# Weights on ScalarE's queue, zero products from the start, and new instruction sequences, in a gated linear attention with a maxout FFN behind it

## Chip, cores and metric

The kernel runs on one core of one Trainium2 chip. The metric is device time in microseconds; the median of three runs of the kernel before is 151.06 us (150.87 to 151.34). Engines are named as in the profile: PE (TensorE, matrix products), PEld (its weight loads), DVE (VectorE), ACT (ScalarE), POOL (GpSimd) and SP (SyncE, which here only requests transfers). Transfers can be requested from SP and from ACT; SPq and ACTq are the rows of these requests.

## What is computed

For each of 4 batches and 8 heads a 48 × 48 state is decayed row by row and gets an outer product added at each of 768 steps; its product with q is the attention's output. The outputs of all heads side by side (3072 tokens of 384) go through a maxout of three matrices and a last matrix.

```python
B, H, S, D = (4, 8, 768, 48)
for t in range(S):
    state = alpha[:, :, t, :, None] * state + einsum('bhd,bhe->bhde', k[:, :, t], v[:, :, t])
    y[:, :, t] = einsum('bhd,bhde->bhe', q[:, :, t], state)
x = y.transpose(0, 2, 1, 3).reshape(B * S, H * D)          # 3072 x 384
h = maximum(maximum(x @ w1, x @ w2), x @ w3)               # 3072 x 768
out = h @ w_out                                            # 3072 x 384
```

Inputs and output are float32. alpha lies between 0.8 and 1.0.

## The kernel before

The work is cut into 24 *units*: 128 time steps of one batch, all 8 heads. Unit u is time block u // 4 of batch u % 4, and two units make a load group n (`load`, line 301): alpha, q, k and v of both, in one transfer each, or one per unit for the first four groups. In the names of the steps, "load a 0 8" is alpha of unit 1, "load a 1 0" that of unit 2.

For each unit the attention is done in chunk form: logarithm of alpha on ACT (`decay`, L402); running sums of it along time by a product with a triangular matrix on PE ("cums", L442); two exponentials of these on ACT (ep and en, L447 and L450); q and k scaled by them on POOL or DVE (L454); v scaled on ACT or POOL (L461, L464); both turned on PE ("turn", L483) and copied to SBUF (L490); "scores" on PE (L499), masked on DVE ("LA", L504); outputs from scores, v and the carried state Z on PE ("outs", L542 and L545), scaled to 16 bits (xb, L556 and L558), turned ("x turn", L572) and copied (xT, L577). `state` carries Z on.

The FFN uses that max(a, b, c) = a + max(0, b − a, c − a). So the kernel casts w1 and w_out to 16 bits on ACT (L333), makes wd = w2 − w1 and w3 − w1 on DVE or POOL (`subs`, L341), and folds w1·w_out into one 384 × 384 matrix: w1 is turned on PE ("w1 turn", L366), copied by ACT (w1T, L372), multiplied with w_out on PE ("fold", L383), and copied by ACT (w1o, L390). Then `ffn` needs two expansions ("grow", L642) per token instead of three, a relu on ACT (L653), a max on DVE (L658), and one contraction ("shrink", L678) over the 384 x's and the 768 h's together. Single units are taken for the first four and last two, pairs else.

Each weight matrix comes in two pieces, columns 0 to 255 and 256 to 767 (rows for w_out): 384 KB and 768 KB (`weights`, L327). All four matrices are requested by SP. "weights g p" is piece p of matrix g in the order w1, w2, w3, w_out.

The program is recorded as *steps*, each with the engines that may do it, and then issued in the order of a written table `ORDER`; `PICK` says where a step takes its second engine, and `BANKS` which of 8 PSUM banks each intermediate gets. So every engine does its work in exactly the order of that table, and waits for data where it must. The tables were the result of a planner that is no part of the kernel.

"zeros" are products of a state tile that holds zeros, written to a PSUM bank that nothing reads (`warm`, L586). There are 27, the first of which waits for k of unit 1 (`reads` of `("qk", hq[u], w)`); they keep TensorE busy where it has nothing else.

Of the kernel before, what the change touches and what calls it, by code (L numbers as in the profile page):

```python
# [17 lines left out]
SIG = 128.0  # L18

# [4 lines left out]
WARM = (1, 1, 27)  # L24
# [55 lines left out]
)  # L80
BANKS = (
# [9 lines left out]
)  # L91
PICK = {
# [8 lines left out]
}  # L101


TRANSFERS = ("load", "weights", "cross", "store")
BEHIND = mybir.DependencyInfo(mybir.DependencyClass.NoSync, mybir.DependencyReason.DATA)
HARD, HARD_LOAD, HARD_LATE, LATE_FROM = 0.5, 1.8, 1.5, 3

# [662 lines left out]
```

## Time and profile before

| | before |
|---|---|
| median of 3 runs | 151.06 us (150.87 to 151.34) |
| the profiled execution | 150.59 us |
| its span, first to last instruction | 148.8 us |
| busy: PE / DVE / ACT / POOL | 133.9 / 106.9 / 90.5 / 52.5 us |
| read from HBM / written | 23.69 / 4.72 MB |

Line numbers in the profile are those of the listing above. "out<-in" names the tiles an instruction writes and reads. The busy time of PE counts pipelined products up to a modelled end; the columns of a stretch are its length, each engine's busy time with the count of its instructions, the granted clock of TensorE (1.00 is full), the busy share of the 16 DMA engines, and GB/s. The share can pass 1, since packets overlap.

### The profile page before, as it was taken

The numbers are of one execution on the slowest core, as the hardware profiler recorded it, in microseconds if no ns is written. First come the engines' busy times: TensorE is split into PE (matmuls) and PEld (weight loads), VectorE is DVE, ScalarE is ACT, GpSimd is POOL, SyncE is SP. The second block draws the span as 40 slices with busy tenths as digits, with TensorE's granted clock in tenths as the row PEclk, the third lists the DMA queues.
The fourth block names the chain that finished last, engine by engine and source line by source line (L and its number), as shares of the span: only waits on it lengthen the run. The fifth ranks groups of instructions, "written<-read, shape, count | busy, mean of one in ns | idle before, by whom it ended". The sixth has DMA issues, their size and how long they took to land.

```text
span 148.8 us, 4162 instructions
## 1 busy us (share of the span) xinstructions
PE 133.9 (90%) x1683; PEld 104.6 (70%) x1683; DVE 106.9 (72%) x186; ACT 90.5 (61%) x184; POOL 52.5 (35%) x75
## 2 busy tenths in 40 slices
PE   0575297999999999999999999999999999999991
PEld 0233266968787886888787797787878877689781
DVE  7239318487998898979697779998578878584140
ACT  3531976948667587797746686745475844554331
POOL 0050041202523414840597709448029290170000
PEclk9999659999999999999999999999999999999999
DMA  5999999999999999999999999899998999704322
GB/s 115 205 225 322 202 341 269 283 267 173 223 208 219 237 220 210 248 184 250 266 266 263 185 197 250 163 215 269 177 232 160 243 325 189 147 4 131 109 82 79
DMA packets 116131, 31.07 MB, mean 209 GB/s; under 512 B 109712, under 2 KB 114960, under 8 KB 116112
## 3 DMA queue, kind: packets, MB, share of 16 engines
q1 hardware_dynamic: 83888, 21.17, 69.7%
q10 hardware_dynamic: 32224, 9.64, 28.7%
q8 instruction: 13, 0.21, 0.6%
q14 instruction: 6, 0.05, 0.1%
HBM read 23.69 MB, written 4.72 MB: 191 GB/s over the span
## 4 chain that ended last, share of the span: by engine, by line
PE 85%; SPq 5%; DMA 4%; ACT 2%; DVE 2%; issue 0%; ACTq 0%
PE psum L642 33%; PE psum L678 24%; PE psum L499 5%; PE psum L483 4%; SPq L308 4%; DMA vn<-in_v_dram 4%; PE psum L545 3%; PE psum L572 3%; PE psum L442 3%; PE psum L542 2%; PE psum L604 2%; PE psum L383 2%; PE psum L586 2%; PE psum L412 1%; DVE wd L341 1%; ACT w1h L333 1%
## 5 line engine op out<-in xcount | busy, mean ns | idle before, releaser
L642 PE MATMUL psum<-xT,wd 128*128 128x256 f16 (+1 forms) x540 | 54.4, 251 | 0.9 <-DVE wd L341 0.9
L642 PEld LDWEIGHTS <-wd 128*128 128x128 f16 x540 | 42.9, 98 | 6.9 <-DVE wd L341 1.7
L658 DVE TENSOR_TENSOR hT<-psum,hT 128x512 f16<-128x512 f32 (+1 forms) x39 | 24.3, 644 | 10.3 <-PE psum L642 4.7
L504 DVE TENSOR_TENSOR LA<-psum,c 128x1024 f16<-128x1024 f32 x24 | 28.6, 1219 | 3.1 <-PE psum L499 2.5
L653 ACT ACTIVATE hT<-psum 128x512 f16<-128x512 f32 (+1 forms) x39 | 21.5, 570 | 14.6 <-PE psum L642 13.6
L678 PE MATMUL psum<-wo,hT 128*128 128x384 f16 (+1 forms) x150 | 27.7, 320 | 0.0
L617 POOL TENSOR_TENSOR Z<-U,G 48x192 f16<-48x192 f32 x29 | 16.4, 572 | 12.5 <-DVE U L611 11.4
L678 PEld LDWEIGHTS <-hT 128*128 128x128 f16 x150 | 14.5, 98 | 8.9
L454 POOL TENSOR_TENSOR qk<-qn,ep 128x384 f16<-128x384 f32 x11 | 10.9, 998 | 15.1 <-ACT ep L447 13.3
L678 PE MATMUL psum<-w1o,xT 128*128 128x384 f16 (+1 forms) x75 | 15.8, 319 | 0.0
L450 ACT ACTIVATE en<-psum 128x384 f32<-128x384 f32 x24 | 11.9, 495 | 4.3 <-PE psum L442 3.8
L402 ACT ACTIVATE la<-an 128x384 f16<-128x384 f32 (+1 forms) x16 | 10.8, 689 | 5.7 <-DMA an<-in_alpha_dram 5.7
L454 POOL TENSOR_TENSOR qk<-kn,en 128x384 f16<-128x384 f32 x8 | 8.3, 1042 | 16.6 <-ACT en L450 12.7
L556 ACT ACTIVATE xb<-psum,c 128x384 f16<-128x384 f32 x16 | 9.1, 582 | 8.0 <-PE psum L545 5.8
L447 ACT ACTIVATE ep<-psum 128x384 f32<-128x384 f32 x24 | 11.7, 496 | 2.6 <-DVE qk L454 0.9
L693 ACT COPY ob<-psum 128x384 f32<-128x384 f32 (+1 forms) x18 | 8.3, 468 | 7.8 <-PE psum L678 5.1
L442 PE MATMUL psum<-la,c 128*128 128x384 f16 x24 | 7.8, 347 | 5.6 <-ACT la L402 5.5
L461 ACT ACTIVATE v<-vn,c 128x384 f16<-128x384 f32 x14 | 8.3, 614 | 6.2 <-DMA vn<-in_v_dram 6.2
L545 PE MATMUL psum<-v,LA 128*128 128x48 f16 x192 | 11.1, 186 | 0.0
L611 DVE TENSOR_TENSOR U<-psum,Z 128x384 f32<-128x384 f32 x16 | 8.5, 551 | 3.1 <-PE psum L604 2.5
L545 PEld LDWEIGHTS <-LA 128*128 128x128 f16 x192 | 9.8, 98 | 0.6 <-issue 0.2
L464 POOL TENSOR_SCALAR v<-vn,c 128x384 f16<-128x384 f32 x10 | 6.3, 635 | 9.4 <-DMA vn<-in_v_dram 9.0
(61 smaller groups left out, 189.6 us busy)
## 6 DMA issues: line engine op xcount, KB each, us to landing
out_dram<-ob ACTq DMA_DIRECT2D x20, 192.0 KB, 3.3
an<-in_alpha_dram SPq DMA_DIRECT2D x7, 384.0 KB, 6.6
ws<-in_moe_w_dram SPq DMA_DIRECT2D x3, 768.0 KB, 6.1
kn<-in_k_dram SPq DMA_DIRECT2D x5, 384.0 KB, 6.5
vn<-in_v_dram ACTq DMA_DIRECT2D x5, 384.0 KB, 6.6
an<-in_alpha_dram SPq DMA_DIRECT2D x8, 192.0 KB, 4.0
kn<-in_k_dram SPq DMA_DIRECT2D x8, 192.0 KB, 4.4
qn<-in_q_dram ACTq DMA_DIRECT2D x4, 384.0 KB, 5.3
```

What stands on the lines that cost most here:

```text
L402: lambda e, lo=lo * H, hi=hi * H: nc.scalar.activation(out=la[:, lo:hi, :D], in_=an[:, lo:hi, :], func=AFT.Ln, scale=1.0 / CDEC),
L442: nc.tensor.matmul(live[Lk], tri, la[:, hs, :D], start=True, stop=True)
L447: lambda e: nc.scalar.activation(out=ep, in_=live[Lk], func=AFT.Exp),
L450: lambda e: nc.scalar.activation(out=en, in_=live[Lk], func=AFT.Exp, scale=-1.0),
L454: lambda e, w=w, x=x, d=d: engines[e].tensor_mul(qk[:, w, :, :D], ld[x][n % LOADED][:, hs], d),
L504: lambda e: nc.vector.tensor_mul(LA.rearrange("p a b t -> p (a b) t"), live[Ak].rearrange("p a (b t) -> p (a b) t", t=P), maskA.unsqueeze( ...
L545: nc.tensor.matmul(yp[:, 2 * j + p, :], LA[:, p, j, :], v16[:, 2 * j + p, :], start=(cb == 0), stop=True, skip_group_check=True)
L617: lambda e, rows=rows, cols=cols: engines[e].tensor_mul(Zn[rows, :, cols], (Us[u % 3] if cb else live[pk])[rows, :, cols], G[rows, i * NP: ...
L642: nc.tensor.matmul(live[gk][:, jj, :], wd[:, kt, g, j * P:(j + 1) * P], xT[:, kt, :], start=(kt == 0), stop=(kt == NFT - 1))
L653: lambda e, h=h, gk=gk: nc.scalar.activation(out=h, in_=live[gk], func=AFT.Relu),
L658: lambda e, h=h, gk=gk: nc.vector.tensor_max(h, live[gk], h),
L678: nc.tensor.matmul(live[ok][:, cols], a[:, i * P:(i + 1) * P], w[:, cols], start=(kt == 0), stop=(kt == nk - 1))
```

## The change

Five edits, made together.

- `weight_options` gets ACT as second engine, and `PICK` takes it for all eight weight pieces. They are requested in the order w1 large, w_out small, w1 small, w_out large, w2 large, w2 small, w3 large, w3 small, between ACT's own instructions.
- The loads on SP start with q of unit 0, alpha of units 0, 1 and 2, k of 0, alpha of 3; all of units 0 and 1 comes before the rest of units 2 and 3. Units 2 and 3 (third and fourth) are worked on after the first eight expansions, and the three fold steps stand ahead of the first expansion.
- `warm` is called before unit 0's outputs, makes 44 zero products instead of 27, and the first depends on nothing but its zeros.
- The tile of zeros is the first that DVE clears, ahead of the other tiles.
- `ORDER`, `BANKS` and `PICK` are replaced as wholes. POOL does 81 steps of the table instead of 71, DVE 159 instead of 166.

The diff without the tables:

```diff
-WARM = (1, 1, 27)
+WARM = 44
...
 def weight_options(share, cast):
     if cast:
         return [("POOL", 0.6 + 0.4 * share, 0, 3.7 * share, 0.2)]
-    return [("SP", HARD, 0, 3.25 * share + 0.1, 0.6)]
+    return [("SP", HARD, 0, 3.25 * share + 0.1, 0.6), ("ACT", 0.45, 0, 3.25 * share)]
...
     hq, ht = rotate(QKS, MORE[0]), rotate(QKTS, MORE[1])
+    nc.vector.memset(Zs[1][0], 0.0)
     for t in las:
         nc.vector.memset(t[:, :, D:], 0.0)
     for t in qks[:QKS]:
         nc.vector.memset(t[:, :, :, D:], 0.0)
-    for zz in Zs:
-        for t in zz:
-            nc.vector.memset(t, 0.0)
+    for t in Zs[0] + Zs[1][1:]:
+        nc.vector.memset(t, 0.0)
...
-    def warm(u, w, count):
+    def warm(count):
...
             plan.step(f"zeros {i}", [("PE", 0.163)], 90.0, zeros,
                       banks=[("wm", 0)] if i == 0 else [],
-                      reads=([("qk", hq[u], w)] if u >= 0 else []) if i == 0 else [("wm", 0)],
+                      reads=[("wm", 0)] if i else [],
                       writes=[("wm", 0)] if i in (0, count - 1) else [])
...
-            if u == WARM[0]:
-                warm(*WARM)
+            if u == 0:
+                warm(WARM)
```

Of the tables, the first line of `ORDER`, by numbers of steps:

```diff
-    4, 8, 9, 5, 6, 0, 10, 12, 34, 7, 32, 1, 11, 2, 123, 65, 127, 82, 84, 128, 129, 83, 64, 131,
+    2, 0, 4, 8, 1, 12, 78, 34, 65, 64, 140, 40, 32, 113, 85, 94, 86, 87, 126, 66, 116, 68, 105,
```

What stands on ScalarE before, around the two casts of w1 (w1h) on whose end TensorE's turns of w1 wait; ws0 is w1, v1 and v2 are scaled v, ep and en exponentials, xb the attention's output in 16 bits:

```order
L402 ACTIVATE la0_82<-an0_66 128x8x48
L461 ACTIVATE v1_101<-vn0_78,c32_62 128x384
L402 ACTIVATE la1_83<-an1_67 128x8x48
L450 ACTIVATE en0_88<-psum_177 128x384
L447 ACTIVATE ep0_85<-psum_177 128x384
L333 CAST w1h_148<-ws0_150 128x3x512
L461 ACTIVATE v2_102<-vn1_79,c32_62 128x384
L333 CAST w1h_148<-ws0_150 128x3x256
L447 ACTIVATE ep0_85<-psum_177 128x384
L490 COPY qkT0_107<-psum_177 128x1024
L556 ACTIVATE xb1_116<-psum_177,c32_62 128x384
L372 COPY w1T_149<-psum_177 128x768
```

What stands there now (ws1 to ws3 are w2, w3 and w_out; lines are two higher in the new kernel):

```order
L335 CAST w1h_148<-ws0_150 128x3x512
L329 DMA ws3_153<-in_moe_w_out_dram 128x4x384
L329 DMA ws1_151<-in_moe_w2_dram 128x3x512
L335 CAST w1h_148<-ws0_150 128x3x256
L420 ACTIVATE e0_141<-psum_177,c32_62 128x16
L449 ACTIVATE ep2_87<-psum_177 128x384
L329 DMA ws1_151<-in_moe_w2_dram 128x3x256
L374 COPY w1T_149<-psum_177 128x768
L329 DMA ws2_152<-in_moe_w3_dram 128x3x512
L335 CAST wo16_155<-ws3_153 128x768
L329 DMA ws2_152<-in_moe_w3_dram 128x3x256
L374 COPY w1T_149<-psum_177 128x768
```

Five requests of weights came in between, both scalings of v and the copy of a turned unit went to other engines, and the small cast of w_out (wo16) moved up from behind the first relus.

What stands on VectorE before, from the last masking ahead of the first subtraction (wd) to the last; ws1 and ws2 are w2 and w3:

```order
L504 TENSOR_TENSOR LA0_112<-psum_177,c16_61 128x1024
L577 COPY xT0_120<-psum_177 128x3x128
L341 TENSOR_TENSOR wd_154<-ws1_151,w1h_148 128x3x512
L577 COPY xT0_120<-psum_177 128x3x128
L454 TENSOR_TENSOR qk3_94<-qn1_71,ep0_85 128x8x48
L490 COPY qkT3_110<-psum_177 128x1024
L504 TENSOR_TENSOR LA0_112<-psum_177,c16_61 128x1024
L341 TENSOR_TENSOR wd_154<-ws2_152,w1h_148 128x3x512
L341 TENSOR_TENSOR wd_154<-ws2_152,w1h_148 128x3x256
```

What stands there now:

```order
L506 TENSOR_TENSOR LA0_112<-psum_177,c16_61 128x1024
L506 TENSOR_TENSOR LA1_113<-psum_177,c16_61 128x1024
L343 TENSOR_TENSOR wd_154<-ws1_151,w1h_148 128x3x512
L579 COPY xT0_120<-psum_177 128x3x128 x2
L343 TENSOR_TENSOR wd_154<-ws2_152,w1h_148 128x3x512
L343 TENSOR_TENSOR wd_154<-ws2_152,w1h_148 128x3x256
```

The subtraction from w2 stands ahead of both x's, and nothing of the fourth unit is left between the subtractions: its product with q went to GpSimd, its copy and its masking went behind the first four maxima.

More of the change, by code (lines that the diff above doesn't have):

```diff
@@ L18 @@
 SIG = 128.0
+TRANSFERS = ("load", "weights", "cross", "store")
+BEHIND = mybir.DependencyInfo(mybir.DependencyClass.NoSync, mybir.DependencyReason.DATA)
 NBANKS = 8
@@ L35 @@
 ORDER = (
[44 rows of a table removed]
[44 rows of a table added]
 )
 BANKS = (
[9 rows of a table removed]
[9 rows of a table added]
 )
 PICK = {
[8 rows of a table removed]
-}
-TRANSFERS = ("load", "weights", "cross", "store")
-BEHIND = mybir.DependencyInfo(mybir.DependencyClass.NoSync, mybir.DependencyReason.DATA)
[10 rows of a table added]
+}
 HARD, HARD_LOAD, HARD_LATE, LATE_FROM = 0.5, 1.8, 1.5, 3
```

120 rows, old and new, of tables (BANKS, ORDER, PICK) are left out of this document.

## Prediction

> **What bounds the kernel now.** I read the page first, then stretches of the span, then the chain that ended last. The page:
>
> ```profile
> span 148.8 us, 4162 instructions
> PE 133.9 (90%) x1683; PEld 104.6 (70%) x1683; DVE 106.9 (72%) x186; ACT 90.5 (61%) x184; POOL 52.5 (35%) x75
> PE 85%; SPq 5%; DMA 4%; ACT 2%; DVE 2%; issue 0%; ACTq 0%
> ```
>
> TensorE is busy for 90% of the span and holds 85% of the last chain; no other engine comes near. Where are the missing 10%? The stretches, with TensorE's busy time, its granted clock and the DMA share:
>
> ```profile
> core 0: us, PE busy (x), PEclk, DMA share, GB/s
> 0.00:5.50 5.50, 0.00 (x0) 1.00 0.73 143
> 5.50:9.40 3.90, 3.78 (x12) 1.00 1.10 217
> 9.40:13.50 4.10, 3.00 (x38) 1.00 1.02 290
> 13.50:17.70 4.20, 0.00 (x0) 0.79 1.03 216
> 17.70:22.10 4.40, 4.39 (x44) 0.50 1.02 328
> 22.10:25.70 3.60, 2.71 (x42) 0.91 1.15 288
> 25.70:33.80 8.10, 8.07 (x104) 1.00 0.99 266
> 33.80:145.80 112.00, 111.95 (x1449) 1.00 1.01 200
> ```
>
> From 25.7 to 145.8 TensorE idles for 0.08 us in all. So the time is decided by how much of its work is left at 25.7, and everything before is a front in which TensorE is empty, or busy with zero products, or at clock 0.50, while the DMA share is 1.0 and more from 5.5 on. The chain through this front:
>
> ```profile
> 8.65 5.77 DMA vn<-in_v_dram
> ...
> 14.51 0.61 ACT v L461
> ...
> 16.29 1.37 ACT w1h L333
> ...
> 17.71 0.82 PE psum L366 x6
> ...
> 23.97 1.68 DVE wd L341
> ...
> 25.69 1.18 PE psum L642 x18
> ...
> 27.03 0.17 PE psum L572 x3
> ...
> 28.91 0.16 PE psum L586
> 29.07 0.45 PE psum L483 x8
> ...
> 30.34 0.36 PE psum L499 x8
> 30.70 3.03 PE psum L383 x18
> ...
> 35.60 0.20 PE psum L545 x8
> ```
>
> A load of v, queued on SP with a weight piece, lets ScalarE go on at 14.51; it casts w1, TensorE turns it (L366), VectorE subtracts w1 from w2 (L341), and at 25.69 the first expansion (L642) starts. The lower rows give the price of each TensorE step at full clock; the product w1·w_out (L383) costs 3.03 and comes after five expansions now.
>
> **The change, part by part.** *What TensorE has done when its expansions start.* Up to its first expansion the new order holds the three products of L383 (3.03) more than the old, and the third unit's turn 0.45, scores 0.36, outputs 0.20 and x turn 0.17 less: 3.03 − 1.18 = 1.85 us ahead. Behind that point stand five zero products instead of four: 0.16 back. All else after it is the same work in another order. So the new kernel ends where the old one does if its first expansion starts at 25.69 + 1.85 − 0.16 = 27.4, provided TensorE stays full afterwards; each microsecond earlier is a microsecond gained. The term to find is that start.
>
> *The transfers.* Rates while loads alone, then a weight piece alone, are moved, and two waits on loads:
>
> ```profile
> 6.00:9.00 3.00, 1.00 1.08 211
> 10.50:11.90 1.40, 1.00 0.99 369
> ```
>
> ```profile
> 4.96 0.94 ACT L402 ACTIVATE la<-an 128x384 f16<-128x384 f32 x2 [2.05 <-DMA an<-in_alpha_dram]
> ...
> 8.79 0.52 ACT L402 ACTIVATE la<-an 128x384 f16<-128x384 f32 x1 [0.69 <-DMA an<-in_alpha_dram]
> ```
>
> A load of one unit is 196.6 KB, at 211 GB/s 0.93 us; a weight piece of 786 KB takes 2.13 at 369, the smaller of 393 KB 1.07. The second load is awaited at 4.96 and the sixth at 8.79: the n-th lands at 3.1 + 0.93 n. (By this the ninth load behind a large piece lands at 13.6; the row has 14.51, so the fit may be 0.9 early.) The DMA engines are full either way, so putting the weights on a second queue makes no bytes faster; it changes who goes first. How two queues share is not seen with weights in this trace. Bounds: the weights wait for all loads in flight, or they push ahead of all loads. I take turns, one transfer each, and both ends move the start below by about a microsecond. The first large piece of w1 goes ahead of the fourth load, so a of the third unit lands at 3.1 + 4 × 0.93 + 2.13 = 9.0, and of the fourth unit (sixth load) at 10.8. ScalarE requests w_out's small and w1's small piece behind the logarithm of 9.0: the latter lands after eight loads at 3.1 + 7.4 + 2.13 + 2 × 1.07 = 14.8. In the same way w_out's large piece lands at 17.9, w2's large piece at 20.9, its small one at 22.9, w3's at 26.0 and 28.0.
>
> *ScalarE's row of work.* Its prices:
>
> ```profile
> 6.46 0.49 ACT L450 ACTIVATE en<-psum 128x384 f32<-128x384 f32 x1 [0.57 <-PE psum L442]
> ...
> 16.18 1.47 ACT L333 CAST w1h<-ws 128x1536 f16<-128x1536 f32 x1
> ...
> 18.06 0.83 ACT L333 CAST w1h<-ws 128x768 f16<-128x768 f32 x1
> ...
> 21.44 0.80 ACT L372 COPY w1T<-psum 128x768 f16<-128x768 f16 x1
> ...
> 25.20 0.30 ACT L418 ACTIVATE e<-psum,c 128x16 f32<-128x16 f32 x1
> ...
> 26.79 1.46 ACT L333 CAST wo<-ws 128x1536 f16<-128x1536 f32 x1
> ...
> 29.43 0.86 ACT L333 CAST wo<-ws 128x768 f16<-128x768 f32 x1
> ```
>
> Logarithm at 9.0 (half of 0.94), 0.57 for the cumulative product, five exponentials at 0.49 and one logarithm: the large cast of w1 runs from about 12.9 to 14.4. The small cast waits for 14.8. From there: 0.83, e 0.30, an exponential 0.49, w1T 0.80, cast 0.86, w1T 0.80, exponential 0.49, w1T 0.80, cast 1.46, together 6.8: at 21.6 w_out stands in 16 bits and L383 can start. TensorE then has 3.03 + two x turns 0.34 + outputs 0.20 + four zero products 0.64 = 4.2 before its first expansion: 25.8. The subtraction from w2 (1.68 from 20.9) is long done, so the cover that hides it is the product of L383. The third matrix is not covered so well: 26.0 + 1.68, and about half of that for the small piece after 28.0, ends at 28.9, while four expansions at 0.5 (1.18 for two and a bit of overlap) reach 27.8 and two more 28.8: 0.15 lost.
>
> *Requests on ScalarE.* How long a request holds its issuer:
>
> ```profile
> 10.77 2.87 SPq L308 DMA_DIRECT2D vn<-in_v_dram  x1
> ...
> 16.63 0.49 SPq L308 DMA_DIRECT2D vn<-in_v_dram  x1
> ```
>
> ```profile
> 58.65 0.40 ACTq L308 DMA_DIRECT2D kn<-in_k_dram  x1
> ```
>
> On ScalarE 0.40, beside the instruction started just before it (a cast, an exponential, a copy), so seven of the eight requests cost nothing. The last, w3's small piece, is made with four others of its queue still on their way, as SP's was at 10.77, and behind it wait the copies of w1T, the cast of w_out and all that follows. Bounds 0 and 2.4 (2.87 − 0.49); nearer the lower end, since the first of the four lands at 17.9, just when the request is due: 0.4. SP is rid of eight requests, worth nothing while the DMA engines are full.
>
> *Zero products from the first microsecond.* Six run at once, then TensorE waits for the first logarithm; the rest fill gaps. At half clock:
>
> ```profile
> 6.22 3.06 PE L586 MATMUL psum<-Z 128*128 128x384 f16 x9
> ```
>
> About 0.32 each instead of 0.16. Between the large cast of w1 and L383 stand 19 of them with three turns of w1 (half of 0.82 each at full clock), two unit turns, two scores and one output: 19 × 0.16 + 3 × 0.41 + 2 × 0.45 + 2 × 0.36 + 0.20 = 6.1 us at full clock, from 14.4 to 20.5, which ScalarE's work to 21.6 hides. If the clock stays halved until 20, 5.6 us do only 2.8 of it, and L383 starts at 20 + 3.3 = 23.3, 1.7 late. Bounds 0 and 1.7; I take 0.35, nearer the lower end: the trace shows full clock after 3.9 us without a pause (5.5 to 9.4), but also 0.50 after 4.2 idle us and through the 4.4 busy us from 17.7.
>
> Sum: 25.8 + 0.15 + 0.4 + 0.35 = 26.7 against 27.4, a gain of 0.7 us: span 148.1. The profiled execution took 150.59 for its span of 148.8 and the median of the runs is 151.06, so 149.9 for a like execution and 150.4 for a median.
>
> **The rivals.** *Clock (slower).* The six early zero products last 6 × 0.32 = 1.9 us, then comes a pause of some 3 (the logarithm needs the third load, after 5.9); from 9 to 13 TensorE is busy in pieces, and idle again for over a microsecond until the cast at 14.4 is through. If full clock needs 3.4 to 3.9 unbroken microseconds, it comes only near 20, L383 starts 1.7 us late as above, and the first expansion moves to 26.7 − 0.35 + 1.7 = 28.05, 0.65 behind 27.4: 151.7. [...] For the rival: the pauses; against: from 14.4 on TensorE has no pause left. It decides if the clock is still 0.5 at 19.
>
> *Late third and fourth unit (slower).* With the weights in turn, the fourth unit's q is the fifteenth load: 3.1 + 15 × 0.93 + 12.8 for all weights = 29.9, and its v, the twentieth, lands at 34.5. Now it is earlier:
>
> ```profile
> 27.83 0.97 DVE L454 TENSOR_TENSOR qk<-qn,ep 128x384 f16<-128x384 f32 x1 [0.17 <-DMA qn<-in_q_dram]
> ```
>
> GpSimd makes both products of this unit now, after one another and before v of the third. TensorE's own work reaches the fourth turn at about 34.5 and its outputs at 38, so I expect this to pass by 1 to 2 us; if loads are served behind weights, or the fit is 0.9 early as above, each later unit's turn waits 0.5 to 1, and the loads of the sixth unit, asked by ScalarE between its own work, repeat it. Price 1 to 3 us off the gain: 151.4 to 153.4.
>
> *More gain.* No clock trouble, no held request, weights ahead: first expansion at 25 to 25.8, a gain of 1.6 to 2.4, 148.7 to 149.5.
>
> **How the numbers follow.** What a measurement can tell from no change is 0.3%, 0.45 us: faster is below 150.6, slower above 151.5. The forecast has 0.45 (149.5 to 151.2: two thirds faster, the rest same and a little), more gain 0.12, the clock 0.16, late units 0.27. Faster: 0.33 + 0.12 + 0.02 = 0.47. Same: 0.12 + 0.03 = 0.15. Slower: 0.13 + 0.25 = 0.38. The range reaches from the middle of "more gain", 148.8, to the end of the late units, 153.4. Both signs are likely; the forecast's own range is 149.5 to 151.2.
>
> **What would show it.** In the new trace, whose lines are two higher: L385 before the first L644, starting near 22, and the first L644 between 25.8 and 27.4; casts of w1 from 12.9 and of w_out ending near 21.6; no idle microsecond of TensorE after that. The clock rival is right if PEclk is 0.5 until about 20 and the zero products last 0.32 there; the late units, if TensorE waits behind GpSimd's products (L456) or v (L466) between 30 and 60. A held request shows as an ACTq row of L329 over 1 us. If TensorE is full from 26 on and the time is still not shorter, my count of the work ahead is wrong.

## The result, and the profile after

The changed kernel is slower: 154.8 us median (154.29 to 156.48) against 151.2 (150.87 to 151.34), ratio 1.029, 95% interval 1.023 to 1.035. On a second chip it took 154.9 against 152.1, ratio 1.020 (1.015 to 1.026). The ratios here and below leave out executions more than 1.5% above the fastest of their kernel, four of the six in e1. The profiled execution took 154.41, its span is 3.8 us longer than before. The page of the changed kernel, its first lines and the chain by engine:

```profile
span 152.6 us, 4192 instructions
PE 138.7 (91%) x1700; PEld 106.5 (70%) x1700; DVE 104.9 (69%) x179; ACT 88.8 (58%) x181; POOL 63.2 (41%) x85
PE 73%; DVE 10%; DMA 8%; ACT 3%; issue 2%; SPq 1%; POOL 0%; ACTq 0%; DVEq 0%; POOLq 0%
```

TensorE was on the last chain for 85% of it and is now for 73%; VectorE came from 2 to 10. The share of busy time, 91%, hides this, since the zero products count as busy. The front in the chain that ended last (start, duration):

```profile
12.90 1.37 ACT w1h L335
...
21.29 1.23 DVE LA L506
...
23.27 0.97 PE psum L385 x6
...
27.69 4.05 DVE wd L343 x2
```

The large cast of w1 runs from 12.9, as reckoned. But the product w1·w_out (L385) starts behind VectorE's masked copy LA of unit 1, at 23.1 and not near 22, and the first expansion at 27.22. Behind it the chain goes at once to VectorE, to the subtraction of the third matrix. The stretches from there on, TensorE alone:

```profile
core 0: us, PE busy (x), PEclk, DMA share, GB/s
27.20:36.00 8.80, 7.59 (x105) 1.00 1.01 200
36.00:45.00 9.00, 8.11 (x139) 1.00 1.19 222
45.00:60.00 15.00, 14.67 (x212) 1.00 1.18 216
60.00:80.00 20.00, 19.24 (x253) 1.00 1.10 203
80.00:149.00 69.00, 68.68 (x857) 1.00 0.90 179
```

The differences add to 3.5 us of idle time, where the old kernel had 0.08 from its first expansion on. What ended it (us in total, times, longest), from 27.3 to 149:

```profile
PE psum L644 <- DVE wd L343: 1.2, 2, 0.7
PE psum L574 <- DVE xb L560: 0.8, 1, 0.8
PE psum L501 <- DVE qkT L492: 0.6, 1, 0.6
PE psum L547 <- POOL v L466: 0.3, 1, 0.3
PE psum L485 <- DVE Z L619: 0.3, 1, 0.3
PE psum L544 <- DVE Z L619: 0.2, 1, 0.2
```

In the old kernel the same view has no row at all from 26.5 to 145.8. To weigh kernels against each other I also use a count of my own, called the excess: for each step of TensorE the time from its start to the start of the next, less what the quickest steps of its kind take, summed from the first expansion to the last step. It is 3.2 us before and 7.2 after; 1.5 of it stands at the third matrix, 1.2 at the zeros tile (42.8 and 43.7), 0.5 at v of unit 4 (49.0), 0.9 at unit 8's output (69.6). It is larger than the idle times of the list, as it also has pauses too short for the list and what slower steps lose. With that the loss closes: start 27.22 − 25.69 = +1.53, useful work left −1.95, one zero product more +0.17, excess +4.06, together 3.81.

Three of these places in the rows. VectorE's subtraction of the third matrix (start, duration, count at the end), in the changed kernel:

```profile
27.60 4.12 DVE L343 TENSOR_TENSOR wd<-ws,w1h 128x1536 f16<-128x1536 f32 x2
```

GpSimd at the same time, in the same timeline:

```profile
27.43 1.00 POOL L456 TENSOR_TENSOR qk<-qn,ep 128x384 f16<-128x384 f32 x1 [1.19 <-DMA qn<-in_q_dram]
28.39 2.52 POOL L456 TENSOR_TENSOR qk<-kn,en 128x384 f16<-128x384 f32 x1
30.87 1.72 POOL L456 TENSOR_TENSOR qk<-qn,ep 128x384 f16<-128x384 f32 x1
```

And the subtraction in the kernel before:

```profile
31.95 2.62 DVE L341 TENSOR_TENSOR wd<-ws,w1h 128x1536 f16<-128x1536 f32 x2
```

The two subtractions take 4.12 beside GpSimd's products and took 2.62 before; the products take 2.52 and 1.72 instead of 1.00. The zeros tile and v of unit 4, in TensorE's timeline of the changed kernel:

```profile
42.60 0.33 PE L588 MATMUL psum<-Z 128*128 128x384 f16 x1
...
43.74 0.61 PE L485 MATMUL psum<-c,qk 128*128 128x128 f16 x8 [0.31 <-DVE Z L619]
44.93 0.40 PE L501 MATMUL psum<-qkT 48*128 48x128 f16 x8 [0.58 <-DVE qkT L492]
...
49.56 0.21 PE L547 MATMUL psum<-v,LA 128*128 128x48 f16 x2 [0.33 <-POOL v L466]
```

The zero product at 42.60 reads the tile that the state Z of unit 0 is to overwrite. So VectorE's Z waits for it, as VectorE's timeline shows:

```profile
42.97 0.72 DVE L619 TENSOR_TENSOR Z<-psum,G 48x192 f16<-48x192 f32 x2 [1.21 <-PE psum L588]
```

Behind Z in VectorE's row stands the copy qkT for which TensorE waits.

### The profile page after: what moved, and what is told of

Same layout as the page of the kernel before. It is cut to its first block, busy times and chain, and to the rows that moved or that the text cites. A ratio compares the mean times of both kernels' runs of the same rounds, so it can differ in the third digit from the quotient of the medians.

```text
span 152.6 us, 4192 instructions
## 1 busy us (share of the span) xinstructions
PE 138.7 (91%) x1700; PEld 106.5 (70%) x1700; DVE 104.9 (69%) x179; ACT 88.8 (58%) x181; POOL 63.2 (41%) x85
## 3 DMA queue, kind: packets, MB, share of 16 engines
HBM read 23.69 MB, written 4.72 MB: 186 GB/s over the span
## 4 chain that ended last, share of the span: by engine, by line
PE 73%; DVE 10%; DMA 8%; ACT 3%; issue 2%; SPq 1%; POOL 0%; ACTq 0%; DVEq 0%; POOLq 0%
PE psum L644 24%; PE psum L680 21%; PE psum L485 5%; DMA an<-in_alpha_dram 4%; DMA kn<-in_k_dram 4%; PE psum L501 4%; PE psum L547 3%; DVE LA L506 3%; PE psum L588 3%; DVE wd L343 3%; PE psum L574 2%; PE psum L444 2%; PE psum L544 2%; PE psum L606 2%; PE psum L385 2%
## 5 line engine op out<-in xcount | busy, mean ns | idle before, releaser
L644 PE MATMUL psum<-xT,wd 128*128 128x256 f16 (+1 forms) x540 | 53.1, 251 | 1.4 <-DVE wd L343 1.2
L644 PEld LDWEIGHTS <-wd 128*128 128x128 f16 x540 | 42.8, 98 | 6.5 <-DVE wd L343 1.5
L660 DVE TENSOR_TENSOR hT<-psum,hT 128x512 f16<-128x512 f32 (+1 forms) x39 | 24.4, 644 | 7.1 <-PE psum L644 4.9
L466 POOL TENSOR_SCALAR v<-vn,c 128x384 f16<-128x384 f32 x16 | 9.9, 622 | 35.7 <-DMA vn<-in_v_dram 29.3
L619 POOL TENSOR_TENSOR Z<-U,G 48x192 f16<-48x192 f32 x23 | 12.0, 527 | 13.9 <-DVE U L613 11.7
L456 POOL TENSOR_TENSOR qk<-qn,ep 128x384 f16<-128x384 f32 x12 | 12.7, 1059 | 10.6 <-ACT ep L449 6.0
L456 POOL TENSOR_TENSOR qk<-kn,en 128x384 f16<-128x384 f32 x14 | 15.5, 1113 | 1.0 <-ACT en L452 0.9
L588 PE MATMUL psum<-Z 128*128 128x384 f16 x44 | 13.5, 422 | 1.1 <-DVE Z L279 1.1
L558 ACT ACTIVATE xb<-psum,c 128x384 f16<-128x384 f32 x14 | 8.2, 583 | 6.4 <-PE psum L547 5.9
L579 ACT COPY xT<-psum 128x384 f16<-128x384 f16 x16 | 7.4, 480 | 7.4 <-PE psum L574 7.4
```

Source lines behind the costliest of these rows:

```text
L456: lambda e, w=w, x=x, d=d: engines[e].tensor_mul(qk[:, w, :, :D], ld[x][n % LOADED][:, hs], d),
L588: nc.tensor.matmul(live["wm"], zero[:, :P], zero, start=True, stop=True)
L619: lambda e, rows=rows, cols=cols: engines[e].tensor_mul(Zn[rows, :, cols], (Us[u % 3] if cb else live[pk])[rows, :, cols], G[rows, i * NP: ...
L644: nc.tensor.matmul(live[gk][:, jj, :], wd[:, kt, g, j * P:(j + 1) * P], xT[:, kt, :], start=(kt == 0), stop=(kt == NFT - 1))
L660: lambda e, h=h, gk=gk: nc.vector.tensor_max(h, live[gk], h),
```

## The experiments

Four theories were open. The order: the loss lies in the places just named, where the new sequences put a step too late or two engines against each other. The queue: weights on ScalarE's queue push the loads back. The clock: TensorE's clock comes up late. And the zero products cost or bring something by themselves. All edits are to the changed kernel unless said otherwise; a number in `ORDER` is a step, and `PICK` sends a step to its second engine.

**e1_no_late_zeros.** The five zero products behind the first expansion.

```diff
-plan.step(f"zeros {i}", [("PE", 0.163)], 90.0, zeros,
+plan.step(f"zeros {i}", [("PE", 0.163)], 90.0, zeros if i not in (10, 34, 22, 42, 43) else lambda e: None,
```

> The changed kernel without the five zero products that stand behind the first expansion (they change no output). Theory, the new sequences lose the time in places that can be named, and these products are one: they take 5 x 0.16 = 0.8 us of a full TensorE, and the last two read the zeros tile that Z 0 0 on VectorE is to overwrite, which the trace shows as waits of 0.48 and 0.75 us at 42.8 and 43.7: the run ends 1.2 to 2.0 us earlier, near 153. Rival, the weights on ScalarE's queue push the loads back and TensorE waits for data whatever the products do: no more than 0.3 us earlier. Rival, the products keep the clock up: without them the clock falls after 27 and the run is longer.

Ratio 1.010 (0.997 to 1.023), times from 151.7 to 156.1. The profiled execution is one of the longer ones, and shows why they spread. TensorE's timeline from 24 to 30:

```profile
26.44 0.41 PE L547 MATMUL psum<-v,LA 128*128 128x48 f16 x8 [2.75 <-POOL v L466]
...
29.84 1.36 PE L644 MATMUL psum<-xT,wd 128*128 128x128 f16 x20
```

Its stretches there (length, busy and instructions, granted clock, DMA share, GB/s):

```profile
24.00:26.00 2.00, 0.00 (x0) 1.00 1.13 262
26.00:28.00 2.00, 1.56 (x13) 0.65 0.59 119
28.00:30.00 2.00, 2.00 (x11) 0.50 1.02 203
```

TensorE was early, waited 2.75 us for v of unit 0, and then had half its clock for 3.4 us (26.6 to 30.0). Behind the first expansion the waits of 0.48 and 0.75 at the zeros tile are gone: VectorE's Z, at 43.29, has no idle time before it, and the rows of 0.6 for qkT and 0.3 for Z are missing from TensorE's list. So this part of the theory holds by the trace; the time alone doesn't settle it.

**e2_sub_early.** VectorE's larger third-matrix subtraction (47) ahead of the transposed copy of unit 0 (125).

```diff
-309, 305, 125, 10, 9, 16, 13, 14, 11, 18, 20, 17, 15, 21, 47, 46, 298,
+309, 305, 47, 125, 10, 9, 16, 13, 14, 11, 18, 20, 17, 15, 21, 46, 298,
```

> The changed kernel with one step moved: VectorE subtracts the larger part of the third matrix ahead of the transposed copy of unit 0, at about 24.8, where its piece has landed (24.7) and VectorE is idle. Theory: the second halves of the first expansions no longer wait for L343 (0.87 and 0.66 us in the trace), the run ends 1.0 to 1.5 us earlier, near 153.5. Rival, loads behind the weights set the end: the wait moves to GpSimd's products of unit 2 and 3 and at most 0.3 us is gained.

Ratio 1.014 (1.007 to 1.022), where the changed kernel has 1.020 to 1.029: shorter by 0.6 to 1.5% (1.0 to 1.5 us, 0.7 to 1.0%, were expected), which the intervals don't make certain. Its profiled execution had the same late v (landed 26.4, first expansion 31.5) and can't show the place undisturbed.

**e3_qk2_on_dve.** Unit 2's products on VectorE: are the subtractions long because of GpSimd?

```diff
+PICK: 147: 1, 148: 1
```

> The changed kernel with the two products of unit 2 (q and k, L456) on VectorE behind the subtractions in place of GpSimd beside them. Theory, VectorE and GpSimd slow each other when both run: the two subtractions take 1.75 and 0.95 us again in place of 2.45 and 1.75, together 2.7 in place of 4.1, the waits before the second halves shrink by about 1, and the run ends 0.5 to 1.2 us earlier. Rival, the subtractions are long because of something else (their operands, the transfers into the staging tile): they stay at 4.1, VectorE has 1.1 more to do, and the run is equal or up to 1 us longer.

VectorE around the subtractions:

```profile
26.62 2.62 DVE L343 TENSOR_TENSOR wd<-ws,w1h 128x1536 f16<-128x1536 f32 x2
...
30.56 1.28 DVE L456 TENSOR_TENSOR qk<-kn,en 128x384 f16<-128x384 f32 x1
```

GpSimd's next product, in the same timeline:

```profile
30.43 0.99 POOL L456 TENSOR_TENSOR qk<-qn,ep 128x384 f16<-128x384 f32 x1 [5.17 <-DMA qn<-in_q_dram]
```

Without GpSimd 2.62 again; and the product of k, 0.55 on VectorE alone, takes 1.28 where GpSimd's product began just before it. So the two engines hold each other up: shown. (0.55 is the product of q at 29.16, of the same shape.) The ratio is 1.016 (1.007 to 1.025). TensorE's waits for the subtraction, 1.2 us, are gone from its list, but a wait of 0.8 (0.99 of excess) is new before the transposes of unit 2, whose product was now late.

**e4_v_early.** The request for v of unit 4 (19) earlier on ScalarE.

```diff
-166, 22, 143, ... 121, 171, 19, 178,
+166, 22, 19, 143, ... 121, 171, 178,
```

> The changed kernel with the request for v of unit 4 moved on ScalarE's queue from about 42.2 to about 37.3 us, behind that for q of unit 5. Theory: v lands near 43 in place of 48.8, GpSimd's cast of it no longer holds the output product of unit 4 (0.49 us), and the run ends 0.3 to 0.6 us earlier. Rival, the transfers share a full path: v comes early but another load comes late by as much, and the time is the same within 0.3.

1.021 (1.013 to 1.030), no difference that can be told. v landed in time and its wait of 0.49 went, but one of 0.48 stood at 57 in its place, behind a product on VectorE that had waited 0.57 us for a load of q: the rival.

**f1_v0_early.** What e1 and e2 showed by accident: v of unit 0 (3), last of its kind on SyncE, goes to ScalarE's queue ahead of w_out's second piece.

```diff
+PICK: 3: 1
```

> The changed kernel with one request moved between the queues: v of unit 0 is asked for by ScalarE ahead of the second piece of w_out, in place of last of its kind on SyncE. Theory A: in the changed kernel this load is pushed behind the weights and lands between 22.9 and 26.4; where it lands after 25 the output product of unit 0 leaves TensorE idle for 2 to 4 us and the granted clock is 0.5 for the 3 us behind that (seen in the profiled executions of the first two experiments: first expansion at 29.8 and 31.5 in place of 26.2 to 27.2). With v early it lands by 18, no window between 24 and 34 shows a clock under 0.9, the first expansion starts at 25.0 to 27.0, and the times lie within 1 us of each other, at 153 to 154.5. Theory B: the idle stretch has another cause (weights, the cast of w_out): it is still there, and the times spread over 2 us as before.

Ratio 1.006 (1.003 to 1.009). v lands at 17.1, and no stretch from 24 to 34 shows a clock under 1.00, as theory A had it; but the times still spread from 152.0 to 155.8, where A had them within 1 us. Why v was late is seen in the DMA queues of the changed kernel from 15 to 24 us, while it was on its way (packets, MB, share of 16 engines; q10 is ScalarE's, q1 SyncE's):

```profile
q10 hardware_dynamic: 1734, 2.74, 89.4%
q1 hardware_dynamic: 1904, 0.36, 21.1%
```

Both queues move about as many packets, but a packet of weights is 1,580 bytes in the mean and one of loads 189, so the weights get nine tenths of the engines' time and 7.6 times the bytes. The counts are not always so near: from 12 to 15 us the loads had 1,786 packets and 56.5% of the engines' time, the weights 546 and 57.6%. v of unit 0 lands 13 to 16 us after its request in this kernel (at 22.9 to 26.4), 6.2 after it in the old one.

**f2_all_mended.** All named places at once.

```diff
+PICK: 3: 1
-ORDER: 125, ... 47, 46     171, 19, 178     386, 487, 277
+ORDER: 47, 125, ... 46     22, 19, 143      386, 277, 487
+zero products 10, 34, 22, 42, 43 left out
```

> The changed kernel with all named places mended: no zero products behind the first expansion, the larger third-matrix subtraction ahead of the transposed copy of unit 0, v of unit 0 early on ScalarE's queue, v of unit 4 early, and the scaled copy of unit 8's output (L560) ahead of a maximum on VectorE (the wait of 0.92 us at 69.6). Theory, the loss lies in these places: the excess of TensorE behind the first expansion falls from 7.2 to 3.5 or 4.0 us, with 0.8 of zero products gone and the first expansion at 25.5 to 27, so that the span is 146.5 to 148.5, the time 148.3 to 150.3: 0 to 2 us under the kernel before. Rival, each mended place hands its wait to the next (a load, a bank): the excess stays above 5.5 and the time above 151.5.

Ratio 1.003 (0.999 to 1.006), median 152.3, excess 6.3: the rival's numbers. Two of my moves were wrong, as TensorE's waits show:

```profile
PE psum L644 <- DVE xT L579: 1.2, 1, 1.2
PE psum L574 <- DVE hT L660: 0.8, 1, 0.8
```

The subtraction, waiting for its piece until 26.0, now held back the copy of unit 0 behind it; and unit 8's transposes need the maximum (L660) as well as the scaled copy, so a swap of these two only changed the name of the releaser.

**f3_weights_on_sp.** The queue alone undone.

```diff
-PICK: 32: 1, 34: 1, 36: 1, 37: 1, 38: 1, 39: 1, 40: 1, 42: 1
```

> The changed kernel with the eight weight requests back on SyncE's queue, at their places in the plan's order. Rival 1, the weights on ScalarE's queue cost time by pushing the loads back: the run ends over 1 us earlier than the changed kernel, under 153.4. Theory, the queue is not what costs: the waits at 28.7, 42.8, 43.7 and 69.6 stay (they hang on the order), the weights land later as they share one queue with the loads, the first expansion starts at 27 to 30, and the run is 0 to 3 us longer than the changed kernel.

Ratio 1.015 (1.009 to 1.021). The first expansion starts at 26.05 and v of unit 0 lands at 18.2, but the waits of the sequence stay:

```profile
PE psum L574 <- DVE xb L560: 0.8, 1, 0.8
...
PE psum L501 <- DVE qkT L492: 0.6, 1, 0.6
```

and others join them; the excess is 8.8. The median, 154.7, is over the 153.4 of the first rival, and the first expansion is earlier than the theory's 27 to 30. The queue is not the main cause.

**f4_before_no_late_zeros.** The kernel before, without its four zero products behind the first expansion.

```diff
+zero products 2, 13, 17, 26 left out
```

> The kernel before without its four zero products behind the first expansion (steps 2, 13, 17 and 26 of them). Theory, behind the first expansion TensorE is full and a zero product costs its own 0.16 us there: the run ends 0.5 to 0.8 us earlier, ratio 0.995 to 0.997. Rival, they fill stretches in which TensorE would wait anyway: no difference (within 0.2 us).

1.000 (0.997 to 1.004): the rival. There they stand where TensorE would have waited anyway; the excess rose from 3.2 to 4.4 in the profiled execution.

**g1_mended_again.** The second try: the copy of unit 0 on ScalarE, so that the subtraction needn't pass it, and the product of k of unit 10 (336) behind both the maximum (487) and the copy (277).

```diff
+PICK: 3: 1, 125: 1
-ORDER: 171, 19, 178    210, 27, 251    344, 336, 343    487, 277, 384
+ORDER: 22, 19, 143     30, 27, 238     344, 343         487, 277, 336, 384
+zero products 10, 34, 22, 42, 43 left out
```

> The changed kernel without zero products behind the first expansion, with v of unit 0 early on ScalarE's queue, v of units 4 and 6 asked for earlier, and two different moves against the second mended kernel: the transposed copy of unit 0 goes to ScalarE (there it stood behind the subtraction on VectorE and cost 1.33 us at 26.3), and the product of k of unit 10 goes behind the maximum and the scaled copy on VectorE (a swap of the last two alone left the wait of 0.92 us before the transposes of unit 8, which need both). Theory: both waits go, the excess behind the first expansion is 3.5 to 4.5 us, the span 146.8 to 148.0 and the time 148.6 to 149.8, ratio 0.98 to 0.99 to the kernel before. Rival, the waits move to the third matrix (its larger piece lands at 26.0 and its subtraction ends near 27.8) and to loads: 1 to 2 us of them come back, ratio 0.99 to 1.005.

150.1 against 151.2, ratio 0.991 (0.988 to 0.995): 0.9% under the kernel before, and under the changed one. The first expansion is at 25.26. The excess, 4.9, is above the theory's 4.5 and the time above its 149.8; part of the rival came true, with 0.5 us of waiting at the third matrix.

**g2_k10_later.** The last of these moves alone.

```diff
-344, 336, 343, ... 487, 277, 384
+344, 343, ... 487, 277, 336, 384
```

> The changed kernel with one step moved: VectorE forms the product of k of unit 10 (L456, 1.27 us beside GpSimd) behind the maximum and the scaled copy of unit 8 in place of ahead of them. Theory: the wait of 0.92 us at 69.6 goes whole, no other wait over 0.3 us appears within 5 us behind it, and the run is 0.6 to 0.9 us shorter. Rival: the product of unit 10 is then late for its transposes and the wait comes back there.

Ratio 1.013 (1.007 to 1.018), against 1.020 to 1.029 for the changed kernel. The wait of 0.92 is gone whole and nothing over 0.3 follows (excess from 60 to 80: 0.2 instead of 1.1).

**g3_mended_filled.** The pause ahead of unit 2's sums filled.

```diff
+def gap(e):
+    for _ in range(8):
+        zeros(e)
...
+gap if i == 27 else zeros if i not in (10, 34, 22, 42, 43) else lambda e: None,
```

> As the first kernel of this group, and the one zero product ahead of the sums of unit 2 repeated eight times, so that TensorE has no idle stretch between 7.8 and 9.9 us. Theory: the time at which the clock comes up hangs on how long TensorE has been without a pause; in the traces so far it came up at 11.6, 14.5 or near 19 with the same code ahead of it. With the pause filled it comes up by 12, the first expansion starts at 25.0 to 25.8 in every execution, and the run is 0 to 1.2 us shorter than the first of this group with less spread. Rival: the front is set by the transfers and by VectorE's masked copies, the clock only shifts slack: no difference over 0.3 us.

0.994 (0.990 to 0.998) against 0.991 for g1: no gain, the rival, and not less spread (149.3 to 153.3, against 148.9 to 150.5). In the profiled execution the clock did come up by 12.5, but L385 started at 21.5 and the first expansion at 25.61, no earlier than in g1. That pair doesn't isolate the pause: in g1's profiled execution the clock was up by then too, and its w1 was cast 1.15 us earlier.

**g4_no_first_zeros.** Without the zero products from the first microsecond.

```diff
+zero products 0, 35, 7, 16, 8, 9 left out
```

> The changed kernel without its first six zero products (from 1.1 to 3.0 us). Theory: TensorE is idle for 3 us behind them anyway, so they bring nothing: the clock comes up at the same times as with them, the same within 0.3 us. Rival, the prediction's term for them (0.35 us of front, bounds 0 and 1.7): the sums and transposes ahead of 19 us run longer at the halved clock, the first expansion starts 0.3 to 1.7 us later and the run is as much longer.

1.021 (1.016 to 1.026), the same as with them on the second chip (1.020). In the profiled execution the first short zero product is at 18.6, where those of the changed kernel have it at 18.3 (h0) to 19.1: the clock comes up no later without them. The intervals would not show the 0.35 us of the prediction, but neither the time nor the clock shows any gain.

**h0 to h3.** Front against sequence, two by two on one chip: neither mended, the load of v of unit 0 alone, the places behind the first expansion alone, both.

```diff
 h1_v0_early_again:  +PICK: 3: 1
 h2_behind_mended:   the diff of g1_mended_again without PICK 3: 1
 h3_both:            the diff of g1_mended_again
```

> The changed kernel again, as the ground for the three others on the same chip. Expected 153.8 to 155, ratio 1.018 to 1.030 to the kernel before.

> The changed kernel with only v of unit 0 asked for by ScalarE ahead of the second piece of w_out. Theory A, the late load holds the front in many executions though not in the profiled one: 1.0 to 1.6 us under the first of this group. Theory B, the waits behind the first expansion are the whole loss: within 0.4 us of it.

> The changed kernel with v of unit 0 as late as it was, and the places behind the first expansion mended: no zero products there, the transposed copy of unit 0 on ScalarE, v of units 4 and 6 asked for earlier, the product of k of unit 10 later. Theory A and B alike let these places give 2.0 to 3.2 us; B gives the whole distance to the fourth of this group (4 us), A leaves 1.0 to 1.6 to the load.

> Both together, the first kernel of the group before once more. If the two causes lie one after the other their gains add: 3.5 to 4.5 us under the first of this group, ratio 0.988 to 0.995 to the kernel before. If both mend the same wait, the sum is 1 us short of that.

| | us, median | ratio to before (95%) | excess |
|---|---|---|---|
| h0, changed kernel | 154.9 | 1.020 (1.015 to 1.026) | 7.0 |
| h1, load early | 153.3 | 1.007 (1.003 to 1.010) | 7.0 |
| h2, sequence mended | 151.3 | 0.993 (0.988 to 0.997) | 3.8 |
| h3, both | 150.0 | 0.986 (0.980 to 0.991) | 3.7 |

By the medians the load is worth 1.6 us, the sequence 3.6, both 4.9. By the ratios it is 1.4, 2.8 and 3.5%, or 2.1, 4.2 and 5.3 us, 1 us short of a full sum. Intervals of half a per cent on each ratio don't decide whether the two add or overlap by that 1 us. The sequence's gain is clear of the intervals with v of unit 0 early or late; the load's is clear of them without the mended sequence, and not with it (0.7%). The sequence gave more than the 2.0 to 3.2 us expected. So both cost the changed kernel time, and the sequence more: shown.

That the load acts ahead of the first expansion is seen in h0's own execution, on GpSimd:

```profile
25.52 0.59 POOL L466 TENSOR_SCALAR v<-vn,c 128x384 f16<-128x384 f32 x1 [4.17 <-DMA vn<-in_v_dram]
```

and on TensorE, which waits for that cast:

```profile
26.16 0.36 PE L547 MATMUL psum<-v,LA 128*128 128x48 f16 x8 [0.97 <-POOL v L466]
```

Its first expansion starts at 27.98. In the execution first compared this wait is missing, and the first expansion at 27.22. The profiled executions of h1 and h3 don't show the load's gain: full clock came only near 19 there, and their first expansions start at 27.74 and 27.67, h2's at 27.14. In h2 all waits of TensorE behind the first expansion are small:

```profile
PE psum L547 <- DVE LA L506: 0.3, 1, 0.3
PE psum L544 <- DVE Z L619: 0.2, 1, 0.2
PE psum L644 <- DVE hT L660: 0.2, 1, 0.2
```

The subtractions on VectorE in h2:

```profile
24.93 4.72 DVE L343 TENSOR_TENSOR wd<-ws,w1h 128x1536 f16<-128x1536 f32 x2 [0.20 <-DMA ws<-in_moe_w_dram]
```

They are longer than ever beside GpSimd, 4.72, but start 2.7 us earlier, and no row of TensorE's list waits for them. Order undid what contention did.

## Why the prediction was wrong, by its own steps

**The break-even start held.** 27.4 was the start at which old and new end together, if TensorE stays full. By the trace's count it is 25.69 + 1.95 − 0.17 = 27.47. The start of 27.22 alone would still have been a gain of 0.25 us.

**"Provided TensorE stays full afterwards" is the step that failed.** For the waits behind the first expansion the sum had 0.15 us, at the third matrix; the idle rows show 3.5 us and the excess rose by 4.06. The third matrix itself was mis-sized: its start I had at 26.0, and it was 27.6, although the larger piece had landed at 24.7, because the subtraction stood in VectorE's row behind the copy of unit 0, which TensorE releases only at the end of L385; and its 1.68 was a price from the old order, where the new one has GpSimd form unit 2's products: 4.12 for both. It cost 1.5. The zeros tile (1.2) and unit 8's output (0.9) were not looked for: I counted the five late zero products as 0.16 each of TensorE's time and did not ask who waits for the tile that they read. I read the new order for the front alone and took the rest as "the same work in another order", which it is, but its waits were not the same.

**The start of the first expansion** was 26.7 in the sum, of which 0.15 belongs behind it, at the third matrix. It was 27.2 in the profiled execution, within the 25.8 to 27.4 to look for, and 28.0 in h0's. The casts and requests went as reckoned: the large cast at 12.9, no request on ScalarE over 0.56 us, so the 0.4 for a held one was not spent; the large cast of w_out ended at 22.4, 0.8 late. Two terms were too small. The first is "turns", one transfer each. For the weights they fit (w2's large piece landed at 20.85 for 20.9, w3's at 24.7 for 26.0), but for the loads the bound at which weights push ahead was the near one: from 15 to 24 us the weights took 7.6 times the bytes. v of unit 0, for which I had no term, lands at 22.9 to 26.4 and is worth 1.6 us in the median of h0 against h1. The second is the clock. The zero products in the changed kernel's timeline, four in a row at 18.24 and again at 20.04:

```profile
18.24 1.19 PE L588 MATMUL psum<-Z 128*128 128x384 f16 x4
...
20.04 0.81 PE L588 MATMUL psum<-Z 128*128 128x384 f16 x4
```

Four of them in g1's:

```profile
16.45 0.81 PE L588 MATMUL psum<-Z 128*128 128x384 f16 x4
```

From one zero product to the next it is 0.32 until 19.0 in the one, 0.16 from 13.9 on in the other. That was the clock rival's condition ("still 0.5 at 19"), by the zero products though not by PEclk, which the stretches give as 1.00 there. The rival's "3.4 to 3.9 unbroken microseconds" was an estimate; what the records show in its place is 1.00 after 3.58 busy us (5.54 to 9.12) and after 5.07 (17.71 to 22.78) in the kernel before, after 4.68 (14.32 to 19.00) in the changed one. The product L385 started at 23.11 where g1's started at 21.15. Of these 1.96 us 0.73 had passed before the first turn of w1 (14.32 and 13.59), and 1.23 came behind it. g1 and h3, one kernel, agree: with full clock by 13.6 the way from the first turn to the product took 7.56 us, with full clock from 18.9 it took 8.67. So the clock's price was 1.1 to 1.2, within the bounds of 0 and 1.7, and I had put 0.35. With v late as well, TensorE would have waited there in part anyway, so the two don't simply add.

**The rivals.** Late units was the nearest, "1 to 3 us off the gain" and weights ahead of the loads, but at other units: v of unit 0 and of unit 4, not the fourth unit's q and v. "My count of the work ahead is wrong" is ruled out: TensorE was not full. The time, 154.8, lies beyond the range, because of the waits of the new sequences behind 27 us only those for loads had a rival. In the chances, 0.33 of 0.45 is nearer three quarters than the two thirds said; nothing hangs on it.

## What to carry to other kernels

When a whole instruction order is replaced, a bound read from the old trace ("the bottleneck engine is full from here on") is a property of the old order: walk the new one past the front too, and for each step of the bottleneck engine ask what stands ahead of its producer in that engine's row. Filler work isn't free where it reads a tile that someone is waiting to overwrite: here VectorE's Z waited 1.21 us for the zero product at 42.60, and TensorE 0.31 and 0.58 behind it. And two DMA queues need not share the bytes equally: here, from 15 to 24 us, when both queues moved about as many packets, the loads in packets of 189 bytes had a fifth of the engines' time. The most urgent load of that stream did better on the queue with the large packets (landed at 17.1 instead of 23.8).

## What the runs showed of the hardware

VectorE's subtraction and GpSimd's products, issued side by side, took as long as if one ran after the other. In the rows above: GpSimd's product runs 27.43 to 28.43 at its own 1.00; VectorE's first subtraction, issued at 27.60, ends at 30.05, 1.62 us after that product, close to its own 1.75; the next product, issued at 28.39, ends at 30.91, 0.86 after the subtraction. Each is within 0.15 us of its own time. The order of the table alone didn't fix how they met: two updates of Z on VectorE near 117 took 1.33 in one execution and 2.13 in another (e4) beside the same GpSimd products, and TensorE waited 0.2 or 1.0 there.

The time at which TensorE reached full rate differed with the same code ahead of it, from 11.5 us (e2) over 12.3 (g1) to 19.0 (the changed kernel), while PEclk reads 1.00 throughout. Ahead of these times that 1.00 is no measurement: the trace keeps the granted clock as records with a start and a length, the first of them starts at 11.47 in e2, 12.26 in g1 and 19.00 in the changed kernel, and before it the views print 1.00 with nothing recorded. From one zero product to the next it is 0.32 ahead of these times and 0.16 behind them. The records change 3.41 us or a multiple of it apart (0.50 from 26.6 to 30.0 in e1; in the kernel before 1.00 from 9.12 to 15.95 and 0.50 from there to 22.78, 6.83 each). Counted back from 19.00 in steps of 3.41, an estimate from these spacings, the pause of 1.0 us ahead of the turns of w1 (14.32 in the changed kernel) fell into the stretch from 12.17 to 15.59, in which TensorE was busy for 2.42 us and behind which the zero products stayed at 0.32; they came to 0.16 behind the next, 15.59 to 19.00, busy for all of its 3.41. In e2 and g1 the first record starts ahead of that pause. So the same code had full clock early or late: g1 and h3, one kernel, at 12.26 and 18.91. How much pause such a stretch may hold is not shown. Filling an earlier pause (g3) brought full rate by 12.5 and no time. Behind the pause of 2.75 us in e1 the granted clock was 0.50 for 3.4 us.
